# A pre-norm linear-attention block with a feed-forward layer: other engines, another order and other constants for its front half

## Chip, cores and metric

The kernel runs on one core of one Trainium2 chip. The metric is device time in microseconds (us); the time of a kernel is the median of its runs. The core's engines each take their instructions in the order in which the program lists them: TensorE (PE, matmuls), VectorE (DVE), ScalarE (ACT), GpSimd (POOL), and SyncE (SP), which here only issues DMAs.

## What is computed

```python
x: [1, 2048, 640] bf16        # H = 32 heads of 20
qkv = layernorm(x) @ wqkv     # [640, 1920]
pq, pk = q @ w_phi[h], k @ w_phi[h]                  # 20 x 20 for each head
phi_q = concat(softmax(pq), softmax(-pq)); phi_k likewise
kv = phi_k^T v;  z = sum over s of phi_k             # per head, 40 x 20 and 40
o  = (phi_q @ kv) / (phi_q @ z + 1e-6)
h  = x + o @ wo
out = h + silu(layernorm(h) @ w1) @ w2               # w1 [640, 1728], w2 [1728, 640]
```

## The kernel before

The 2048 rows are 16 tiles `t` of 128 rows. Weights and the whole of `X` stay in SBUF.

**Front.** `w_phi` is folded into the projections first: `phi_blocks` lays the 32 blocks of 20x20 along a diagonal in PSUM (37 small matmuls), `phi_a` and `phi_b` copy them to SBUF, `wk0`, `wk2`, `wk4` transpose `Wk` on PE, `wq0..4` transpose `Wq` by DMA, and `fold` multiplies them into `Wfk` and `Wfq`. Meanwhile `WARM` matmuls on a constant keep PE at work.

**Key phase, for each tile.** `st` (moments of the rows, DVE), `rs` (inverse deviation, POOL), `xn` (normalized rows; DVE for tiles below `XP`, else POOL), `xt` (transposed into `XnT`: on PE with a copy on ACT for tiles below `XD`, else a DMA transpose that SP issues), then `K` (project, PE), `ex` (exponentials, ACT), `su` (their sums, DVE), `rk` (1/sum, ACT), `sc` (scaling, DVE), `V` (project, PE), `ve` (copy, ACT) and `kv` (accumulate in one PSUM tile, PE). `bd0`, `bd1` cut the block diagonal out of it (DVE, with masks built on POOL). The query projections `Q` need `XnT` and `Wfq` alone.

**Attention, for each tile.** `qe` (ACT), `qs` and `qr` (DVE), `qt` (DMA transpose), `D` (PE), `E` (divide, DVE), `ot` (transpose: PE for the first two tiles, then DMA), `G` (output projection, PE), `ga` (residual, DVE), `ls`, `lr`, `hn` (second layer norm), `ht` (transpose).

**Feed-forward, for each tile.** `u` (up, PE), `s` (silu, ACT), `d` (down, PE), `oa` (residual, DVE), `out` (DMA). It starts once all query exponentials are done (`use_late`).

**What sets the order.** No order is written out. Each step is given to `Plan.add` with an engine, an assumed duration, a rank, what it depends on, an earliest time `after` and, for a DMA, an assumed time to landing `lands`. `Plan.run` goes through an imagined time and, of the steps that could begin, takes the one that can begin first (within `SLACK`), by rank among equals; it adds `HOP` between dependent steps. The instructions are emitted in that order, so these numbers decide only the order in each engine's queue. `AHEAD` bounds by how many tiles `D` may run ahead of the feed-forward.

Of the kernel before, what the change touches and what calls it, by code (L numbers as in the profile page):

```python
# [90 lines left out]
def kernel(  # L91
# [77 lines left out]
    nc.sync.dma_start(Wk[:, 0:3], wqkv_v[:, 0:3, D : 2 * D])  # L169
# [57 lines left out]
    def warm():  # L227

        nc.tensor.matmul(  # L229
            kv_ps[:, 0, :], ident[:], ident[:].unsqueeze(1).to_broadcast([P, 4, P]),  # L230
            start=True, stop=True,
        )
# [37 lines left out]
    PA = 380  # L270
    PN = 820
    HEADS = {0: (0, 7), 4: (25, 7), 1: (6, 7), 3: (19, 7), 2: (12, 8)}

    PB = {0: (0, 240, 0), 4: (400, 640, 140), 1: (120, 260, 380), 3: (380, 520, 520), 2: (240, 400, 660)}

    phi = early.tile([P, PN], BF16, name="phi")
    ps_of = {}

    def phi_blocks():
        pp = ps_of["phi"] = ps_pair()  # L280
        nc.tensor.matmul(pp[:, 0, 140:240], SID[:, 0:P], WPH[:, 0:5, :], start=True, stop=True)
        for r, (h0, n) in HEADS.items():
            for h in range(h0, h0 + n):
                at = DH * h - PB[r][0] + PB[r][2]
                b, at = (0, at) if at < PA else (1, at - PA)
                p0 = DH * h - P * r
                nc.tensor.matmul(
                    pp[:, b, at : at + DH], SID[:, P - p0 : 2 * P - p0], WPH[:, h, :],
                    start=True, stop=True,
                )  # L290
# [113 lines left out]
    for t in range(T):  # L404
        ahead = t - 3.2 if t > 0 else -10
        add(f"st{t}", "DVE", 1.06, 10 + ahead, [], lambda t=t: moments(t), after=AT_X[t])
        add(f"rs{t}", "POOL", 0.8, 10 + ahead, [f"st{t}"], lambda t=t: inv_std(t))
        ring = [f"xt{t - 4}"] if t > 3 else []
        if t < XP:
            add(f"xn{t}", "DVE", 0.42, 10 + ahead, [f"rs{t}"] + ring, lambda t=t: normal(t, nc.vector))  # L410
        else:
# [7 lines left out]
        else:  # L419
            add(  # L420
                f"xt{t}", "SP", 1.21, 10 + ahead, [f"xn{t}"],
                lambda t=t: nc.sync.dma_start_transpose(xt(t), xn_.pop(t)[:]), lands=2.6,
            )
            add(f"x{t}", "none", 0.0, 0, [f"xt{t}"], lambda: None)
            if later_loads:
                load = later_loads.pop(0)
                add(f"load{t}", "SP", 0.58, 10 + t, [f"xt{t}"], lambda load=load: nc.sync.dma_start(*load))
# [445 lines left out]
```

## Time and profile before

| | us |
|---|---|
| median of 3 runs (lowest to highest) | 255.53 (253.95 to 257.6) |
| the profiled execution's own time | 254.95 |
| its span, first to last instruction | 253.2 |
| busy in that span: PE, DVE, ACT, POOL | 240.1, 168.3, 109.0, 66.2 |
| granted TensorE clock, mean | 0.998 |

A group's row gives busy time, mean duration of one in ns, and the idle time of its engine just before it with what ended that. A timeline row gives start, duration, engine, line, operation, and in brackets the idle time before it. The chain of work is followed back from the last instruction, at each step to what released it.

### The profile page before, as it was taken

Reading aid. Unit: us, or ns where it says so; the run is one execution under the profiler, and the core shown is the slowest. Engines: PE = TensorE matmul, PEld = TensorE weight load, DVE = VectorE, ACT = ScalarE, POOL = GpSimd, SP = SyncE. Lnnn points to the kernel's source line nnn. Section 1 sums busy time; section 2 is a strip of 40 time slices with the busy share of each in tenths; the row PEclk is TensorE's granted clock in tenths of the full one; section 3 lists DMA queues with packets and bytes.
Section 4 is the critical chain, followed back from the end, with each engine's and each line's share of the span. In section 5 each row is a group of like instructions: output and inputs, shape, how many; then the busy total and the mean of one; then the engine's idle time right before and its main releaser. Section 6 shows DMA issues by size and latency. Waiting matters only on the chain.

```text
span 253.2 us, 6387 instructions
## 1 busy us (share of the span) xinstructions
PE 240.1 (95%) x2689; PEld 192.5 (76%) x2689; DVE 168.3 (66%) x349; ACT 109.0 (43%) x220; POOL 66.2 (26%) x103
## 2 busy tenths in 40 slices
PE   7989898989999899899999999999999999999994
PEld 3966566757677677797897897897898798797972
DVE  2698799895679889898968668667826526502011
ACT  2686676768689757640141141141141141041320
POOL 3269979999600011110200200200200100100000
PEclk9999999999999999999999999999999999999999
DMA  7997974673102825468465267485153213200001
GB/s 201 381 298 219 227 249 86 181 218 54 26 3 52 106 52 67 91 109 127 102 109 107 54 62 149 54 100 111 44 96 72 52 46 63 52 28 28 26 5 49
DMA packets 61302, 26.32 MB, mean 104 GB/s; under 512 B 53786, under 2 KB 60122, under 8 KB 61146
## 3 DMA queue, kind: packets, MB, share of 16 engines
q1 hardware_dynamic: 60624, 25.90, 48.3%
q8 instruction: 21, 0.34, 0.6%
q10 hardware_dynamic: 650, 0.03, 0.2%
q14 instruction: 7, 0.06, 0.1%
HBM read 10.35 MB, written 2.62 MB: 51 GB/s over the span
## 4 chain that ended last, share of the span: by engine, by line
PE 68%; POOL 17%; DMA 6%; ACT 5%; DVE 2%; issue 1%; POOLq 0%; ACTq 0%
PE half L781 24%; PE half L797 23%; POOL xn L386 13%; PE half L671 8%; ACT Eq L463 4%; DMA OT<-O 4%; PE pair L435 3%; PE half L640 3%; DMA XnT<-xn 2%; POOL rs L382 2%; PE half L446 2%; PE kv L229 2%; POOL rs L379 1%; PE pair L303 1%; PE pair L335 1%
## 5 line engine op out<-in xcount | busy, mean ns | idle before, releaser
L791 ACT ACTIVATE shT<-half 128x512 bf16<-128x512 f32 (+1 forms) x64 | 34.7, 544 | 107.9 <-PE half L781 107.9
L781 PE MATMUL half<-HnT,w_sb 128*128 128x128 bf16 x1120 | 66.0, 219 | 0.0
L781 PEld LDWEIGHTS <-w_sb 128*128 128x128 bf16 x1120 | 63.9, 98 | 1.1
L797 PE MATMUL half<-w_sb,shT 128*128 128x320 bf16 x448 | 64.8, 299 | 0.0
L797 PEld LDWEIGHTS <-shT 128*128 128x128 bf16 x448 | 43.0, 98 | 15.7
L435 PEld LDWEIGHTS <-XnT 128*128 128x128 bf16 x360 | 33.7, 98 | 19.2 <-DMA XnT<-xn 6.6
L379 POOL TENSOR_SCALAR rs<-mv 128x1 f32<-128x1 f32 x32 | 9.0, 282 | 148.8 <-DVE mv L375 148.7
L806 DVE TENSOR_TENSOR o_t<-half,X 128x320 bf16<-128x320 f32 x32 | 15.6, 486 | 35.3 <-PE half L797 35.3
L386 POOL TENSOR_SCALAR xn<-X,mv,rs 128x640 bf16<-128x640 bf16 x12 | 32.6, 2722 | 0.2
L374 DVE BATCH_NORM_STATS2 st<-X 128x6 f32<-128x320 bf16 x64 | 28.0, 480 | 4.5 <-DMA X<-in_A_x_dram 4.5
L435 PE MATMUL pair<-Wfk,XnT 128*128 128x320 bf16 x160 | 24.3, 299 | 5.0 <-DMA XnT<-xn 3.5
L478 DVE TENSOR_REDUCE Sk<-Ek 128x64 f32<-128x1280 bf16 x16 | 23.4, 1469 | 5.0 <-ACT Ek L463 5.0
L463 ACT ACTIVATE Ek<-pair 128x640 bf16<-128x640 f32 x32 | 20.7, 699 | 12.2 <-PE pair L435 12.1
L671 PE MATMUL half<-wo_sb,OT 128*128 128x320 bf16 x160 | 24.2, 299 | 1.3 <-DMA OT<-O 1.3
L573 DVE TENSOR_REDUCE Sq<-Eq 128x64 f32<-128x1280 bf16 x16 | 23.5, 1477 | 0.9 <-ACT Eq L463 0.9
L435 PE MATMUL pair<-Wv,XnT 128*128 128x320 bf16 x150 | 22.8, 299 | 0.0
L671 PEld LDWEIGHTS <-OT 128*128 128x128 bf16 x160 | 15.3, 98 | 7.7 <-DMA OT<-O 1.9
L678 DVE TENSOR_TENSOR X<-half,X 128x320 bf16<-128x320 f32 x32 | 15.3, 485 | 6.8 <-PE half L671 6.8
L650 DVE RECIPROCAL Rd<-half 128x16 f32<-128x16 f32 x32 | 7.9, 247 | 17.7 <-PE half L640 17.6
L382 POOL TENSOR_TENSOR rs<-rs,nhalf_t 128x1 f32<-128x1 f32 x32 | 18.2, 569 | 2.7
L463 ACT ACTIVATE Eq<-half 128x320 bf16<-128x320 f32 x48 | 16.7, 469 | 4.4 <-PE half L446 3.4
L446 PE MATMUL half<-Wfq,XnT 128*128 128x320 bf16 x120 | 17.4, 299 | 0.0
(68 smaller groups left out, 195.4 us busy)
## 6 DMA issues: line engine op xcount, KB each, us to landing
out_dram<-o_t SPq DMA_DIRECT2D x16, 160.0 KB, 2.0
w_sb<-in_B_w_dram SPq DMA_DIRECT2D x5, 432.0 KB, 4.5
w_sb<-in_B_w_dram SPq DMA_DIRECT2D x3, 480.0 KB, 4.3
X<-in_A_x_dram SPq DMA_DIRECT2D x1, 1280.0 KB
Wv<-in_A_wqkv_dram SPq DMA_DIRECT2D x1, 800.0 KB, 7.0
Wq<-in_A_wqkv_dram SPq DMA_DIRECT2D x1, 800.0 KB, 8.9
wo_sb<-in_A_wo_dram SPq DMA_DIRECT2D x1, 800.0 KB, 5.2
X<-in_A_x_dram SPq DMA_DIRECT2D x2, 320.0 KB, 5.5
```

What stands on the lines that cost most here:

```text
L374: nc.vector.bn_stats(st[:, i, :], X[:, t, i * HD : (i + 1) * HD])
L382: nc.gpsimd.tensor_tensor(rs_[t][:], rs_[t][:], nhalf_t[:], op=ALU.pow)
L386: eng.tensor_scalar(out=xn_[t][:], in0=X[:, t, :], scalar1=mv_.pop(t)[:, 0:1], scalar2=rs_.pop(t)[:], op0=ALU.subtract, op1=ALU.mult,)
L435: nc.tensor.matmul(ps[:, g, 0:HD], XnT[:, c, t * P : (t + 1) * P], W[:, c, g * HD : (g + 1) * HD], start=(c == 0), stop=(c == C - 1),)
L446: nc.tensor.matmul(ps[:, 0:HD], XnT[:, c, t * P : (t + 1) * P], W[:, c, g * HD : (g + 1) * HD], start=(c == 0), stop=(c == C - 1),)
L463: nc.scalar.activation(E5[:, g, :, b, :], p4, AF.Exp, scale=sign)
L478: nc.vector.tensor_reduce(sk[t][:], ek[t][:].rearrange("p (q f) -> p q f", f=DH), axis=AX.X, op=ALU.add)
L573: nc.vector.tensor_reduce(sq[t][:], eq[t][:].rearrange("p (q f) -> p q f", f=DH), axis=AX.X, op=ALU.add)
L671: nc.tensor.matmul(ps[:, 0:HD], ot[t][:, c, :], wo_sb[:, c, g * HD : (g + 1) * HD], start=(c == 0), stop=(c == C - 1),)
L781: nc.tensor.matmul(p3[:, i, :], w1_sb[:, c, fc * P : fc * P + P], HnT[u][:, c, 0:n], start=(c == 0), stop=(c == C - 1),)
L791: nc.scalar.activation(shT[u][:, f0:f1, 0:n], p3, AF.Silu)
L797: nc.tensor.matmul(ps[:, 0:HD], shT[u][:, fc, k * P : (k + 1) * P], w2_sb[:, fc, g * HD : (g + 1) * HD], start=(fc == 0), stop=(fc == FC - 1),
```

## The change

- POOL's list of normalizations loses two tiles: `xn` of tiles 6 and 11 joins tiles 0 to 3 on DVE. (The short description speaks of four tiles; two change the engine of `xn`, and two more, tiles 2 and 3, have `xt` on PE and ACT instead of a DMA.)
- The 11 loads of `wo`, `w1` and `w2` no longer hang one by one behind the `xt` DMAs; each gets an assumed earliest time of 30 us, 33 us and so on.
- `phi` is made by six matmuls (a replicated identity `REP` times up to eight heads at once), and DVE multiplies the result by a 0/1 mask `own` while it takes it out of PSUM. POOL builds `own`; before, ACT did the two copies.
- `Wk`'s first three chunks are loaded by ACT's queue, behind `w_phi`, instead of SP's.
- The warm-up multiplies a tile set by DVE and not the identity that POOL makes; ten of them instead of nine.
- `Plan`'s numbers change: DMA transposes are assumed to land after 4.7 us (2.6 and 2.7 before; 5.5 instead of 3.5 for `qt`) and to hold SP for 1.6 us (1.21), `HOP` is 0.23 (0.15), `SLACK` 0.05 (0.1), POOL's `xn` 2.75 (2.5), and the ranks of `E`, `ga` and `oa`, `AHEAD` (3.7 to 3.02) and `QLAG` (2 to 1) move.

```diff
-    SLACK = 0.1
-    HOP = 0.15
+    SLACK = 0.05
+    HOP = 0.23
...
+    LEAD = 2.5
+    LAND = 4.7
+    XDVE = (0, 1, 2, 3, 6, 11)
+    LOADS = (30.0, 3.0)
+    XD = 4
+    ROFF = (-4, -9, -5)
...
     nc.scalar.dma_start(WPH[:], A_w_phi.rearrange("h d f -> d h f"))
+    nc.scalar.dma_start(Wk[:, 0:3], wqkv_v[:, 0:3, D : 2 * D])
...
     load_x(0, 2)
-    nc.sync.dma_start(Wk[:, 0:3], wqkv_v[:, 0:3, D : 2 * D])
...
+    warm_t = early.tile([P, 4 * P], BF16, name="warm_t")
+    nc.vector.memset(warm_t[:], 1.0)
...
+    REP = early.tile([DH, H, DH], BF16, name="REP")
+    nc.gpsimd.tensor_copy(REP[:], ident[0:DH, 0:DH].unsqueeze(1).to_broadcast([DH, H, DH]))
...
+    own = early.tile([P, NB, 8, DH], BF16, name="own")
+    nc.gpsimd.memset(own[:], 1.0)
+    nc.gpsimd.affine_select(
+        out=own[:], in_=own[:], compare_op=ALU.is_ge, fill=0.0,
+        base=0, pattern=[[4, NB], [-DH, 8], [0, DH]], channel_multiplier=1,
+    )
...
+                nc.tensor.matmul(
+                    pp[:, i // 3, at : at + n * DH], rep[:, r * P : (r + 1) * P], WPH[:, h0 : h0 + n, :],
+                    start=True, stop=True,
+                )
...
+        nc.vector.tensor_tensor(
+            phi[:, 3 * b : 3 * b + n, 0 : 8 * DH],
+            ps_of["phi"][:, b, 0 : 8 * DH * n].rearrange("p (i f) -> p i f", i=n),
+            own[:, 3 * b : 3 * b + n].rearrange("p i h f -> p i (h f)"), op=ALU.mult,
+        )
...
-        if t < XP:
+        if t in XDVE:
...
-                f"xt{t}", "SP", 1.21, 10 + ahead, [f"xn{t}"],
-                lambda t=t: nc.sync.dma_start_transpose(xt(t), xn_.pop(t)[:]), lands=2.6,
+                f"xt{t}", "SP", 1.6, 10 + ahead, [f"xn{t}"],
+                lambda t=t: nc.sync.dma_start_transpose(xt(t), xn_.pop(t)[:]), lands=LAND,
             )
             add(f"x{t}", "none", 0.0, 0, [f"xt{t}"], lambda: None)
-            if later_loads:
-                load = later_loads.pop(0)
-                add(f"load{t}", "SP", 0.58, 10 + t, [f"xt{t}"], lambda load=load: nc.sync.dma_start(*load))
+    for i, load in enumerate(later_loads):
+        add(f"load{i}", "SP", 1.2, 50, [], lambda load=load: nc.sync.dma_start(*load), after=LOADS[0] + LOADS[1] * i)
```

Three places show what this does to the queues. The first is SP's queue between the loads of the start and the middle of the key phase, before:

```order
L326 DMA_TRANSPOSE WTq<-Wq 128x5x128 x2
L422 DMA_TRANSPOSE XnT<-xn 128x5x128 x2
L326 DMA_TRANSPOSE WTq<-Wq 128x5x128
L427 DMA wo_sb<-in_A_wo_dram 128x5x640
L427 DMA w_sb<-in_B_w_dram 128x1728
L422 DMA_TRANSPOSE XnT<-xn 128x5x128
L326 DMA_TRANSPOSE WTq<-Wq 128x5x128 x2
L422 DMA_TRANSPOSE XnT<-xn 128x5x128
L427 DMA w_sb<-in_B_w_dram 128x1728 x2
```

The same place of SP's queue after the change:

```order
L362 DMA_TRANSPOSE WTq<-Wq 128x5x128 x4
L458 DMA_TRANSPOSE XnT<-xn 128x5x128
L362 DMA_TRANSPOSE WTq<-Wq 128x5x128
L458 DMA_TRANSPOSE XnT<-xn 128x5x128 x3
L463 DMA wo_sb<-in_A_wo_dram 128x5x640
L463 DMA w_sb<-in_B_w_dram 128x1728
```

The first `XnT` transpose is now tile 4's (tiles 2 and 3 have left the queue), and no load of a weight stands ahead of those of tiles 4 to 7. The second place is POOL's queue from tile 5 on (`rs_394` and `xn_414` are tile 5's), before:

```order
L386 TENSOR_SCALAR xn_414<-X_80,mv_342,rs_394 128x640
L379 TENSOR_SCALAR rs_464<-mv_416 128x1
L382 TENSOR_TENSOR rs_464<-rs_464,nhalf_t_101 128x1
L256 MEMSET w2_sb_79 64x640
L386 TENSOR_SCALAR xn_499<-X_80,mv_416,rs_464 128x640
L379 TENSOR_SCALAR rs_531<-mv_480 128x1
L382 TENSOR_TENSOR rs_531<-rs_531,nhalf_t_101 128x1
L257 MEMSET mask_108 128x420
L386 TENSOR_SCALAR xn_557<-X_80,mv_480,rs_531 128x640
```

POOL's queue from tile 5 on after the change:

```order
L422 TENSOR_SCALAR xn_401<-X_80,mv_323,rs_373 128x640
L415 TENSOR_SCALAR rs_453<-mv_393 128x1
L418 TENSOR_TENSOR rs_453<-rs_453,nhalf_t_102 128x1
L267 MEMSET w2_sb_79 64x640
L415 TENSOR_SCALAR rs_475<-mv_456 128x1
L418 TENSOR_TENSOR rs_475<-rs_475,nhalf_t_102 128x1
L268 MEMSET mask_109 128x420
L422 TENSOR_SCALAR xn_496<-X_80,mv_456,rs_475 128x640
```

Tile 6 keeps its `rs` there (`rs_453`) but its `xn` is gone, so that tile 7's `xn` follows that of tile 5. The third place is DVE's queue at the end of the key phase, before (`Sk` and `Ek` are the sums and scalings of the keys, `Sq` the first sums of a query tile, `KVB` the block diagonal):

```order
L478 TENSOR_REDUCE Sk<-Ek 128x64
L491 TENSOR_TENSOR Ek<-Ek,Rk 128x1280
L478 TENSOR_REDUCE Sk<-Ek 128x64
L491 TENSOR_TENSOR Ek<-Ek,Rk 128x1280
L573 TENSOR_REDUCE Sq<-Eq 128x64
L519 TENSOR_TENSOR KVB<-kv,mask 128x5x84
```

DVE's queue there after the change:

```order
L609 TENSOR_REDUCE Sq<-Eq 128x64
L514 TENSOR_REDUCE Sk<-Ek 128x64
L617 RECIPROCAL Rq<-Sq 128x32
L619 TENSOR_TENSOR Rho<-Sq,Rq 128x64
L626 TENSOR_TENSOR Eq<-Eq,Rho 128x32x20
L514 TENSOR_REDUCE Sk<-Ek 128x64
L527 TENSOR_TENSOR Ek<-Ek,Rk 128x1280
L514 TENSOR_REDUCE Sk<-Ek 128x64
L527 TENSOR_TENSOR Ek<-Ek,Rk 128x1280 x2
L514 TENSOR_REDUCE Sk<-Ek 128x64 x2
L527 TENSOR_TENSOR Ek<-Ek,Rk 128x1280 x2
L609 TENSOR_REDUCE Sq<-Eq 128x64 x2
```

The sums of query tile 0 (`Sq`) now stand ahead of the last five key sums, and the rest of its work (`Rq`, `Rho`, `Eq`) ahead of the last four; before, all of it came behind them. On PE, four query projections (`Q0` to `Q3`) now stand ahead of the last `kv`, where there were two.

More of the change, by code (lines that the diff above doesn't have):

```diff
@@ L152, in ps_half_bf16 @@
         return pools["half"].tile([P, 8, P], BF16, name="half")
+    ST1 = 4.9
+    ST2 = 10.4
+    ST3 = 12.8
+    WARM = 10
+    LEAD = 2.5
+    V0 = 3.25
+    WQ = 14.0
+    LAND = 4.7
+    XDVE = (0, 1, 2, 3, 6, 11)
+    LOADS = (30.0, 3.0)
+    XD = 4
+    NE = 4
+    EQT = 3
+    RAMP = 2
+    QSUM = (20, 22, 24)
+    QLAG = 1
+    AHEAD = 3.02
+    NHN = 4
+    NSH = 4
+    ROFF = (-4, -9, -5)
     Wk = early.tile([P, C, D], BF16, name="Wk")
@@ L229, in warm @@
         nc.tensor.matmul(
-            kv_ps[:, 0, :], ident[:], ident[:].unsqueeze(1).to_broadcast([P, 4, P]),
-            start=True, stop=True,
+            kv_ps[:, 0, :], warm_t[:, 0:P], warm_t[:], start=True, stop=True,
         )
     for i in range(WARM):
-        add(f"warm{i}", "PE", 0.42, 3 * R, [], warm, after=1.4)
+        add(f"warm{i}", "PE", 0.42, 3 * R, [], warm, after=1.0)
     for i, v in enumerate(VP):
@@ L269 @@
     NB = 5
[L270 to L276, printed above, removed]
+    BW = 240
+    BLOCKS = (0, 3, 1, 4, 2)
+    HEAD0 = {0: 0, 3: 19, 1: 6, 4: 25, 2: 12}
+    PB = {
+        0: (0, 240, 0), 3: (380, 520, BW), 1: (120, 260, 2 * BW), 4: (400, 640, 3 * BW - 100),
+        2: (240, 400, 4 * BW),
+    }
+    assert all(P * r - DH * HEAD0[r] == 4 * i for i, r in enumerate(BLOCKS))
+    phi = early.tile([P, NB, BW], BF16, name="phi")
+    own = early.tile([P, NB, 8, DH], BF16, name="own")
[4 more added lines that the diff above has]
+    )
+    nc.gpsimd.affine_select(
+        out=own[:], in_=own[:], compare_op=ALU.is_ge, fill=0.0,
+        base=DH - 1, pattern=[[-4, NB], [DH, 8], [0, DH]], channel_multiplier=-1,
+    )
+    nc.gpsimd.memset(phi[:, :, 8 * DH : BW], 0.0)
     ps_of = {}
@@ L280, in phi_blocks, with phi_own @@
         pp = ps_of["phi"] = ps_pair()
[L281 to L286, printed above, removed]
+        rep = REP[:].rearrange("k h d -> k (h d)")
+        for i, r in enumerate(BLOCKS):
+            at = 8 * DH * (i % 3)
+            for h0, n in [(HEAD0[r], min(8, H - HEAD0[r]))] + [(0, 1)] * (HEAD0[r] + 8 > H):
                 nc.tensor.matmul(
-                    pp[:, b, at : at + DH], SID[:, P - p0 : 2 * P - p0], WPH[:, h, :],
+                    pp[:, i // 3, at : at + n * DH], rep[:, r * P : (r + 1) * P], WPH[:, h0 : h0 + n, :],
                     start=True, stop=True,
                 )
-    add("phi", "PE", 1.2, 1, [], phi_blocks, after=AT_WPH, ring=("pair", [["phi_a", "phi_b"]]))
-    add("phi_a", "ACT", 0.5, 1, ["phi"], lambda: act(phi[:, 0:PA], ps_of["phi"][:, 0, 0:PA]))
-    add("phi_b", "ACT", 0.5, 1.1, ["phi"], lambda: act(phi[:, PA:PN], ps_of["phi"][:, 1, 0 : PN - PA]))
+                at += n * DH
+    def phi_own(b):
+        n = 3 - b
+        nc.vector.tensor_tensor(
[3 more added lines that the diff above has]
+        )
+    add("phi", "PE", 0.6, 1, [], phi_blocks, after=AT_WPH, ring=("pair", [["phi_a", "phi_b"]]))
+    add("phi_a", "DVE", 0.6, 1, ["phi"], lambda: phi_own(0))
+    add("phi_b", "DVE", 0.45, 1.1, ["phi"], lambda: phi_own(1))
     Wfk = proj.tile([P, C, D], BF16, name="Wfk")
```

48 lines of the change are left out of this document (17 added, 31 removed).

## Prediction

> **What bounds the kernel now.** First the totals and the chain of work on the profile's page:
>
> ```profile
> span 253.2 us, 6387 instructions
> ...
> PE 240.1 (95%) x2689; PEld 192.5 (76%) x2689; DVE 168.3 (66%) x349; ACT 109.0 (43%) x220; POOL 66.2 (26%) x103
> ...
> PE 68%; POOL 17%; DMA 6%; ACT 5%; DVE 2%; issue 1%; POOLq 0%; ACTq 0%
> ```
>
> PE works in 240.1 of 253.2 us, so all that better order can give back is the 13.1 us in which it doesn't. Yet 17% of the chain lies on POOL, which is busy for a quarter of the span: there must be a stage that POOL bounds. A table of stages shows where (columns: stretch and length, then busy us and instructions of PE, PE's weight loads, DVE, ACT and POOL):
>
> ```profile
> 4.53:13.84 9.31, 9.07 (x116) 7.77 (x115) 6.94 (x17) 5.44 (x9) 2.56 (x6) 1.00 1.05 380
> 13.84:55.70 41.86, 37.29 (x348) 27.06 (x347) 37.23 (x64) 30.27 (x62) 37.63 (x38) 1.00 0.84 211
> 55.70:73.00 17.30, 16.25 (x158) 12.07 (x159) 11.49 (x11) 12.33 (x26) 11.41 (x15) 1.00 0.17 30
> 73.00:104.00 31.00, 29.01 (x260) 21.41 (x258) 26.93 (x60) 24.94 (x61) 1.61 (x4) 1.00 0.46 68
> 104.00:216.00 112.00, 111.54 (x1408) 94.97 (x1406) 78.51 (x185) 26.71 (x49) 10.29 (x26) 1.00 0.49 84
> 216.00:249.90 33.90, 33.82 (x403) 28.20 (x400) 6.81 (x17) 8.03 (x15) 0.79 (x2) 1.00 0.11 30
> ```
>
> PE's idle time is length minus PE busy: 0.24, 4.57, 1.05, 1.99, 0.46 and 0.08 us. So 5.6 us lie in the key phase (13.84 to 73.00), 2.0 in the ramp of the attention, half a microsecond in 146 us of feed-forward. The rest is the start (1.42 us) and the last output (3.3), which the change leaves. PE's timeline names the waits (start, duration, then in brackets the idle time and what ended it):
>
> ```profile
> 27.46 1.53 PE L435 MATMUL pair<-Wfk,XnT 128*128 128x320 bf16 x10 [1.25 <-DMA XnT<-xn]
> ...
> 42.36 1.53 PE L435 MATMUL pair<-Wfk,XnT 128*128 128x320 bf16 x10 [1.16 <-ACT Wfq L344]
> ...
> 56.02 1.53 PE L435 MATMUL pair<-Wfk,XnT 128*128 128x320 bf16 x10 [1.10 <-DMA XnT<-xn]
> ...
> 86.85 0.62 PE L640 MATMUL half<-KVB,EqT 128*128 128x126 bf16 x10 [1.16 <-ACT OT L666]
> ...
> 102.44 1.53 PE L671 MATMUL half<-wo_sb,OT 128*128 128x320 bf16 x10 [0.81 <-DMA OT<-O]
> ...
> 173.53 1.53 PE L671 MATMUL half<-wo_sb,OT 128*128 128x320 bf16 x10 [0.46 <-DMA OT<-O]
> ```
>
> Most end with a DMA transpose that landed late, because its input or its turn on SP came late. All these are waits in the queue's order: PE had other work, but behind.
>
> **The start: -0.3 us.** The chain's first pieces, one piece of the ramp to compare with, and the load that is moved:
>
> ```profile
> 1.42 3.60 PE kv L229 x8
> 5.01 0.20 PE pair L281
> 5.21 0.95 PE pair L287 x36
> 6.16 0.54 PE kv L229
> 6.70 2.13 PE pair L303 x20
> 8.83 0.53 PE pair L393 x5
> ...
> 90.19 0.28 PE half L393 x5
> ```
>
> ```profile
> 1.25 0.42 SPq L169 DMA_DIRECT2D Wk<-in_A_wqkv_dram  x1
> ```
>
> ```profile
> Wk<-in_A_wqkv_dram SPq DMA_DIRECT2D x1, 480.0 KB, 4.7
> ```
>
> Eight warm-up matmuls of 512 columns took 3.60 us, 0.45 each or 0.88 ns a column. The 37 small `phi` matmuls (0.20 + 0.95 = 1.15) become six with 5 x 160 = 800 columns: 0.70. Ten warm-ups take 4.5 us and begin when DVE has filled their tile, between 0.7 us earlier than the 1.42 of now (half of what stands before it) and no earlier; so `phi` would end between 5.9 and 6.6, where the ninth warm-up ended at 6.70. But `Wk`'s first chunks landed at 1.25 + 4.7 = 5.95, and are issued behind `w_phi` now and share the DMA engines with `X`: between 5.9 and 7.2 (all of one 480 KB load at the same rate). I take 0.3 us gained, between a gain of 0.8 and a loss of 0.5. The two copies of `phi` leave ACT and become 800 columns of multiplication on DVE; DVE's share is priced below. POOL's masks stand ahead of `rs` of tile 0:
>
> ```profile
> masks.py:199 POOL TENSOR_SCALAR_AFFINE_SELECT ident<-ident 128x128 bf16<-128x128 bf16 x1 | 0.3, 294 | 0.1
> ...
> L244 POOL TENSOR_SCALAR_AFFINE_SELECT mask<-mask 128x84 f32<-128x84 f32 x5 | 1.4, 284 | 0.0
> ```
>
> ```profile
> 5.75 0.22 POOL L379 TENSOR_SCALAR rs<-mv 128x1 f32<-128x1 f32 x1 [3.15 <-DVE mv L375]
> ```
>
> No row shows a POOL operation of 800 elements. From 84 elements in 284 ns to 128 in 294 gives 0.45 us by the slope, in proportion to the second 1.84. The five new ones (a copy, two fills, two selects) take between 2.2 and 9.2 us. POOL stood idle for 3.15 us ahead of tile 0's `rs`, and the chain has that tile's transpose on PE only at 8.83, some two us after its rows are ready: cover for 5.2 us. I take the slope, being what both rows together say, and cost nothing; the upper end loses 4.0.
>
> **The key phase: -4.4 us.** What POOL does and what moves (groups: busy, mean ns of one):
>
> ```profile
> L386 POOL TENSOR_SCALAR xn<-X,mv,rs 128x640 bf16<-128x640 bf16 x12 | 32.6, 2722 | 0.2
> ...
> L573 DVE TENSOR_REDUCE Sq<-Eq 128x64 f32<-128x1280 bf16 x16 | 23.5, 1477 | 0.9 <-ACT Eq L463 0.9
> ...
> L651 DVE TENSOR_TENSOR O<-half,Rd 128x320 bf16<-128x320 f32 x32 | 15.7, 492 | 1.1
> ...
> L386 DVE TENSOR_SCALAR xn<-X,mv,rs 128x640 bf16<-128x640 bf16 x20 | 8.8, 438 | 1.1 <-POOL rs L382 1.1
> ...
> L590 DVE TENSOR_TENSOR Eq<-Eq,Rho 128x640 bf16<-128x640 bf16 x16 | 7.9, 492 | 0.6
> ...
> L581 DVE RECIPROCAL Rq<-Sq 128x32 f32<-128x32 f32 x16 | 5.5, 342 | 0.1
> ...
> L583 DVE TENSOR_TENSOR Rho<-Sq,Rq 128x64 bf16<-128x64 f32 x16 | 3.6, 225 | 0.5
> ```
>
> ```profile
> 17.32 2.52 POOL L386 TENSOR_SCALAR xn<-X,mv,rs 128x640 bf16<-128x640 bf16 x1
> ...
> 60.55 3.73 POOL L386 TENSOR_SCALAR xn<-X,mv,rs 128x640 bf16<-128x640 bf16 x1
> ```
>
> POOL's first `xn` begins at 17.32 and its last ends at 64.28: 47 us for 12 tiles. Two fewer take 2 x 2.72 = 5.4 us off, so its last would end near 58.8. Then POOL no longer ends last, and what does? DVE. Its idle time, from the same table, is 2.37 + 4.63 + 5.81 = 12.81 us up to 73.00, where its last key scaling ends. It gets more work before that point: two `xn` (0.88), the mask multiplication (800 columns from PSUM at 492 ns for 320: 1.23), and the whole of query tile 0 (1.477 + 0.342 + 0.225 + 0.492 = 2.54), together 4.65 us. What stays of the 12.81? The 5.81 behind 55.70 fall where POOL was last: gone. Of the 7.0 before it, I let 0.5 go with the late transpose at 27.46 and keep 6.5. Then the last scaling comes 12.81 - 6.5 - 4.65 = 1.7 us earlier, and PE has by then done two query projections more, of ten matmuls, each some 1.36 us (a row's 1.53 less the 0.17 us by which the last overlaps the next): 2.7. Sum 4.4. PE itself sets a cap of 5.6 - 0.56 = 5.0, with two tiles' transposes more at 0.28 each. The bounds are 5.0 gained and the loss of the slower rival below.
>
> The SP queue carries this:
>
> ```profile
> 20.48 0.57 SPq L427 DMA_DIRECT2D wo_sb<-in_A_wo_dram  x1
> 21.10 0.52 SPq L427 DMA_DIRECT2D w_sb<-in_B_w_dram  x1
> 21.72 1.47 SPq L422 DMA_TRANSPOSE XnT<-xn  x1
> ```
>
> ```profile
> XnT<-xn SPq DMA_TRANSPOSE x14, 3.0
> ```
>
> Tile 4's rows were ready at 19.84 (17.32 + 2.52), but its transpose was issued at 21.72, behind a `Wq` transpose and two loads, and PE's wait of 1.25 us ended at 27.46. After, four `Wq` transposes end ahead of it and no load stands there: issued at about 20, it lands at 23 to 25.7 (after the median 3.0 or the 5.7 of now). PE asks for it near 24.5: the first key projection begins where the second stage of the table does, at 13.84, and seven projections of 1.36 us, two tiles' transposes and some small matmuls come before tile 4's. The 11 loads still pass SP ahead of tiles 8 to 15; POOL's lead of up to 5 us is their cover, and without it each would cost its 0.5 to 0.6 us of issue. The weights are first read in the ramp, behind 73.
>
> **Ramp and feed-forward: -1.3 us.** Query tile 0 is ready before the key phase ends, so the first attention no longer waits for its sums, ratio and DMA. But DVE was busy for 26.93 of 31 us there, and two first sums (3.0 us) now stand ahead of the block diagonal. I take half of PE's 1.99 us, between all of it and a loss of 1.0 (one more wait like that at 86.85). In the feed-forward I take 0.3 of 0.46, since more of PE's work now stands between a tile's `D` and its `G`. Bounds: 0.46 gained, 1.0 lost.
>
> **The sum.** -0.3 - 4.4 - 1.0 - 0.3 = -6.0 us: the profiled execution of 254.95 (253.2 and 1.75 around it) would give 248.95. It stands 0.58 under the median of 255.53, so by the median **249.5**, 2.3% less. The lowest and highest run lie 1.4% apart, so 2% (250.4 and 260.6) is about what can be told.
>
> **Rivals.**
> - *DVE takes POOL's place* (20%). More of its waits are for ACT (`ex`, `rk`) than for POOL; the full queue of moments then puts them off. With 9.0 us idle instead of 6.5 the key phase gives 1.9, the ramp nothing: 255.53 - 0.3 - 1.9 = 253.3. For it: between 13.84 and 55.70 DVE is busy in 89% already. Against it: PE has four projections as filler.
> - *The array speeds up earlier* (13%). The 20 transposes from 6.70 took 107 ns each; the same five in the ramp take 0.28, 56 ns each. If the many small `phi` matmuls kept the rate low, an unbroken train of ten would raise it before the 25 `Wk` transposes: 25 x 51 ns = 1.3 us more, 248.2. Against it: eight large ones in 3.6 us didn't. The Trainium skill, "TensorE: Matmul & The Clock Gate", section "Part 1: The HAM clock gate", says that the array goes to full rate after about 3.4 us of sustained work in a window that runs freely; the trace agrees only if `phi` counts as a break, and by the rule this case would be the likely one.
> - *The gaps only move* (7%). Landings, not their assumed length, are late: four `Wq` transposes in a row now stand ahead of tile 4's. With the 1.25 us and the like kept and only 1.0 gained: 254.5.
> - *Slower* (5%). One mechanism, in DVE's queue: all its 12.81 us of idle time stay, being ACT's round trips. The 4.65 us more push the last scaling back by as much, and PE's filler gives back 2.7: 255.53 + 1.9 = 257.4. It decides from 12.81 - 4.65 + 2.7 = 10.9 us of idle time on.
>
> **Chances and range.** The forecast has 55%, with its own range 247.9 to 251.2; four fifths of it lie under 250.4. Faster by over 2%: 0.44 + 0.13 = 0.57. Slower by over 2%: 0.03, beyond the slower rival's own time. The rest, 0.40, is within. The range 246.5 to 253.6 takes in the forecast, the array's earlier speed with all of the key phase's cap, and DVE's case; the last two rivals stay out.
>
> **What would show it.** Right: POOL's last `xn` ends near 59 and PE's idle time between 13.84 and 73 is under 2 us; the last `kv` matmuls start near 72 with four query projections done; DVE's idle time up to its last key scaling is 6 to 7 us; feed-forward is as dense as now. Wrong: PE waits for `Ek` scalings (DVE) instead of transposes; `rs` of tile 0 begins after 8 us; the `Wk` transposes run at 56 ns; or PE waits for `OT` again and again behind 104.

## The result and the profile after

| | before | changed |
|---|---|---|
| median of 6 runs, us (lowest to highest) | 254.33 (253.53 to 257.6) | 245.91 (245.57 to 246.99) |
| the profiled execution, us | 254.95 | 245.69 |
| its span, us | 253.2 | 244.0 |

The ratio is 0.968 (95% interval 0.9642 to 0.9717): 8.4 us faster by the medians, 9.3 between the two profiled executions. The forecast was 6.0 faster, 249.5, with a range from 246.5: right in direction, too small in size. The ratio and its interval leave out the run of 257.6, more than 1.5% above the fastest of its kernel; without it the median of before is 253.95 and the gain 8.0.

The same rows of the page as before, now of the changed kernel:

```profile
span 244.0 us, 6342 instructions
...
PE 236.8 (97%) x2669; PEld 191.3 (78%) x2669; DVE 170.7 (70%) x354; ACT 107.1 (44%) x216; POOL 64.1 (26%) x104
...
PE 94%; DMA 2%; DVE 1%; ACT 1%; ACTq 0%; issue 0%
```

POOL's 17% of the chain is gone altogether, though POOL's busy time fell only from 66.2 to 64.1 us. PE's is 94% where it was 68%. The table of stages of the changed kernel (length, then PE, PE's weight loads, DVE, ACT, POOL):

```profile
4.51:13.59 9.08, 7.25 (x86) 5.56 (x84) 7.68 (x19) 4.44 (x7) 4.09 (x12) 1.00 1.07 388
13.59:73.00 59.41, 58.91 (x567) 44.32 (x567) 55.71 (x84) 47.89 (x98) 43.77 (x50) 1.00 0.64 158
73.00:104.00 31.00, 31.00 (x322) 24.55 (x321) 28.85 (x69) 21.98 (x54) 3.17 (x8) 1.00 0.43 81
104.00:216.00 112.00, 112.00 (x1414) 95.63 (x1412) 71.61 (x169) 26.39 (x49) 8.67 (x22) 1.00 0.46 81
```

PE's idle time in the key phase went from 5.62 to 0.50 us, in the ramp from 1.99 to 0.00, in the feed-forward from 0.46 to 0.00. All waits of PE that its timeline still shows before the last output:

```profile
1.51 3.98 PE L241 MATMUL kv<-warm_t 128*128 128x512 bf16 x10 [1.51 <-DVE warm_t L215]
7.33 1.29 PE L339 MATMUL pair<-ident,Wk 128*128 128x128 bf16 x20 [1.38 <-DMA Wk<-in_A_wqkv_dram]
9.37 1.55 PE L371 MATMUL pair<-phi,WTk 128*128 128x240 bf16 x18 [0.19 <-DVE WTk L355]
13.59 1.52 PE L471 MATMUL pair<-Wfk,XnT 128*128 128x320 bf16 x10 [0.24 <-DVE Wfk L380]
32.78 0.56 PE L543 MATMUL kv<-VP,Ek 128*128 128x84 bf16 x10 [0.45 <-DVE Ek L527]
```

From 33 us on PE never waits for data until the end. The longest wait that the kernel before did not have is at 7.33, for the load that was moved to ACT's queue.

**What a wait costs beside its idle time.** The three stages' idle time fell by 7.6 us, the start came 0.25 us earlier, and two more tiles' transposes on PE took 0.56: that makes 7.3 of the 9.2 us of span. Two rows of the changed kernel's timeline, one behind the other, show where more went:

```profile
69.02 1.52 PE L471 MATMUL pair<-Wfq,XnT 128*128 128x320 bf16 x10
70.38 0.55 PE L543 MATMUL kv<-VP,Ek 128*128 128x84 bf16 x10
```

The projection lasts 1.52 us by its row, but the next group begins after 1.36: successive matmuls overlap by 0.16 us in the profile, where the ends of matmuls are modelled, and that much stands as busy time ahead of every wait. Eleven waits of before behind 13.84 became one, which by this estimate is 10 x 0.16 = 1.6 us, so 8.9 of 9.2 are told; the last 0.3 is not.

### The profile page after: what moved, and what is told of

It is laid out like the page before. It is cut to its first block, busy times and chain, and to the rows that moved or that the text cites. A ratio compares the mean times of both kernels' runs of the same rounds, so it can differ in the third digit from the quotient of the medians.

```text
span 244.0 us, 6342 instructions
## 1 busy us (share of the span) xinstructions
PE 236.8 (97%) x2669; PEld 191.3 (78%) x2669; DVE 170.7 (70%) x354; ACT 107.1 (44%) x216; POOL 64.1 (26%) x104
## 4 chain that ended last, share of the span: by engine, by line
PE 94%; DMA 2%; DVE 1%; ACT 1%; ACTq 0%; issue 0%
PE half L817 26%; PE half L833 25%; PE pair L471 20%; PE half L707 9%; PE half L482 6%; PE half L676 3%; PE kv L543 3%; DMA Wk<-in_A_wqkv_dram 2%; PE pair L371 1%; PE kv L471 1%; ACT Ek L499 1%; PE half L429 0%; DVE Wfk L380 0%; DVE Ek L527 0%; PE pair L339 0%; ACT WTk L355 0%
## 5 line engine op out<-in xcount | busy, mean ns | idle before, releaser
L817 PE MATMUL half<-HnT,w_sb 128*128 128x128 bf16 x1120 | 66.9, 219 | 0.0
L833 PE MATMUL half<-w_sb,shT 128*128 128x320 bf16 x448 | 63.5, 299 | 0.0
L415 POOL TENSOR_SCALAR rs<-mv 128x1 f32<-128x1 f32 x32 | 7.6, 238 | 154.3 <-DVE mv L411 154.3
L471 PEld LDWEIGHTS <-XnT 128*128 128x128 bf16 x380 | 36.2, 98 | 13.5 <-issue 0.5
L422 POOL TENSOR_SCALAR xn<-X,mv,rs 128x640 bf16<-128x640 bf16 x10 | 27.9, 2790 | 0.1
L418 POOL TENSOR_TENSOR rs<-rs,nhalf_t 128x1 f32<-128x1 f32 x32 | 19.0, 594 | 2.7
L687 DVE TENSOR_TENSOR O<-half,Rd 128x320 bf16<-128x320 f32 x32 | 15.7, 491 | 1.1
L499 ACT ACTIVATE Eq<-half 128x320 bf16<-128x320 f32 x40 | 14.0, 458 | 3.0 <-PE half L482 3.0
L482 PE MATMUL half<-Wfq,XnT 128*128 128x320 bf16 x100 | 14.7, 299 | 0.0
```

Of the source, the lines that this page charges most:

```text
L418: nc.gpsimd.tensor_tensor(rs_[t][:], rs_[t][:], nhalf_t[:], op=ALU.pow)
L422: eng.tensor_scalar(out=xn_[t][:], in0=X[:, t, :], scalar1=mv_.pop(t)[:, 0:1], scalar2=rs_.pop(t)[:], op0=ALU.subtract, op1=ALU.mult,)
L471: nc.tensor.matmul(ps[:, g, 0:HD], XnT[:, c, t * P : (t + 1) * P], W[:, c, g * HD : (g + 1) * HD], start=(c == 0), stop=(c == C - 1),)
L482: nc.tensor.matmul(ps[:, 0:HD], XnT[:, c, t * P : (t + 1) * P], W[:, c, g * HD : (g + 1) * HD], start=(c == 0), stop=(c == C - 1),)
L499: nc.scalar.activation(E5[:, g, :, b, :], p4, AF.Exp, scale=sign)
L817: nc.tensor.matmul(p3[:, i, :], w1_sb[:, c, fc * P : fc * P + P], HnT[u][:, c, 0:n], start=(c == 0), stop=(c == C - 1),)
```

## Experiments

Times are medians; the ratio is to the kernel before, run on the same chip. "Waits" means the sum of PE's waits behind the first key projection, in key phase, ramp and feed-forward (before: 5.5, 2.0, 0.5; changed: 0.45, 0, 0).

### The two halves of the change, each alone

The kernel before with tiles 6 and 11 normalized on DVE:

```diff
-        if t < XP:
+        if t < XP or t in (6, 11):
```

> The kernel before with one part of the change: tiles 6 and 11 are normalized on DVE. Theory A (POOL's rate of one normalization per 3.9 us bounded the key phase): most of that phase's loss goes, POOL's last normalization ends near 59 us, 249.5 us against 254.3. Theory B (the order was wrong because landings were assumed too short): PE still meets late transposes in its queue, no more than 1.5 us gained, 253.

251.89 us, 0.992 (0.9889 to 0.9948). Waits 3.7, 0.5, 1.1. That is between the two theories (249.5 and 253). POOL lost two tiles, its last `xn` ended at 62.4 instead of 64.28, and PE still met late tiles.

The kernel before with all of the plan's numbers:

```diff
-    SLACK = 0.1
-    HOP = 0.15
+    SLACK = 0.05
+    HOP = 0.23
...
-            add(f"xn{t}", "POOL", 2.5, 10 + ahead, [f"rs{t}"] + ring, lambda t=t: normal(t, nc.gpsimd))
+            add(f"xn{t}", "POOL", 2.75, 10 + ahead, [f"rs{t}"] + ring, lambda t=t: normal(t, nc.gpsimd))
...
-                lambda t=t: nc.sync.dma_start_transpose(xt(t), xn_.pop(t)[:]), lands=2.6,
+                lambda t=t: nc.sync.dma_start_transpose(xt(t), xn_.pop(t)[:]), lands=LAND,
...
```

with SP's holds, `LEAD` (it shifts the ranks of a tile's normalization), the rank and earliest time of `wq`, `QLAG`, `AHEAD` and `ROFF` (the ranks of `E`, `ga` and `oa`) as in the change.

> The kernel before with one part of the change: the plan's numbers alone (landing 4.7 us, hop, slack, durations of SP and POOL, ranks of E, ga, oa, AHEAD, QLAG, LEAD). Theory A: POOL still ends last in the key phase (64 us), only the 2.0 us of the ramp and the 0.5 us of the feed-forward go, with their refills 3 us: 251.3. Theory B: the order fills the key phase's waits with query projections too: 248.

249.5 us, 0.983 (0.9769 to 0.9889). Waits 2.0, 1.4, 0. No work went to another engine, and PE, DVE and POOL run as many instructions as before. ACT runs eight fewer (212 for 220): a query tile that is projected before the PSUM buffers are divided anew gets its exponentials in two instructions and not in four, and four more tiles are. So beside the order in the queues the numbers decide this too. They gain 4.3 us, where relieving POOL gains 1.9. Up to 1.2 of the 4.3 can be the start's (first key projection at 12.62 in this profile, 13.84 before; the array's rate, below); the kernel with the assumed times alone, further down, gains 4.2 without such help.

Both together, without the new `phi`, without tiles 2 and 3 on PE, with `Wk` on SP, the weights' loads behind the `xt` DMAs and the warm-up as before:

> The kernel before with all of the plan's numbers and tiles 6 and 11 normalized by DVE; phi, the loads, XD = 2 and the warm-up as before. Theory 'each part pays for itself on top of the right order': the numbers' 249.5 less 1 to 2, 247.5 to 248.5. Rival 'the numbers had already taken what the tiles on DVE give, and only tiles 2 and 3 on PE pay': 249 to 250. Rival 'the two belong together and the rest is nothing': 246 to 247.

248.76 us, 0.980 (0.9756 to 0.9841). The waits left behind the start (engine, line, what it waited for: sum, times, longest):

```profile
PE kv L509 <- DVE Ek L493: 2.2, 2, 1.3
...
PE pair L337 <- DMA WTq<-Wq: 1.0, 1, 1.0
```

No `XnT` is late any more; what is late is DVE, and one transpose of `Wq`. Its median lies 0.7 under the numbers alone, but the two profiles differ in the start too (first key projection at 13.83 and 12.62, for the array's rate, below): behind it, the one took 233.0 us to the end of its span and the other 235.0.

### Taken from the changed kernel one by one

```diff
-    XDVE = (0, 1, 2, 3, 6, 11)
+    XDVE = (0, 1, 2, 3)
```

> The changed kernel with tiles 6 and 11 normalized on POOL again. Theory A: POOL bounds the key phase again, 4 to 5 us are lost: 250.5 against 245.9. Theory B: query projections fill what POOL leaves open, at most 1 us is lost: 247.

248.59 us, 0.979 (0.9738 to 0.9848): 2.7 more than the changed kernel, between the two theories (250.5 and 247). PE's waits behind the start are not for POOL's tiles:

```profile
PE half L482 <- ACT Eq L499: 1.4, 1, 1.4
PE kv L543 <- DVE Ek L527: 1.0, 1, 1.0
```

```diff
-    XD = 4
+    XD = 2
```

> The changed kernel with tiles 2 and 3 transposed by DMA again and not on PE and ACT. Theory (they kept PE's start of the key phase dense, at 0.56 us of PE's own time): the waits for Wq's and XnT's DMAs between 18 and 20 us come back, 1.0 us lost net, 247. Rival (the query work fills it): 0.5 us gained, 245.4.

248.55 us, 0.979 (0.9744 to 0.9829): 2.6 more. Waits 3.1, 0, 0, of which 2.2 for DVE's `Ek` scalings and 0.7 for ACT.

The plan's numbers of before in the changed kernel (the second diff above, reversed; the landing of `xt` goes to 2.7, where before it was 2.6):

> The changed kernel with the plan's numbers of before (landing 2.7 us, hop, slack, durations of SP and POOL, ranks, AHEAD, QLAG, LEAD). Theory A: the ramp's and the feed-forward's waits come back, 3 us: 249. Theory B: those of the key phase too: 251.5.

253.33 us, 0.997 (0.9935 to 0.9997): 7.4 more, nearly all of the gain, with POOL's ten tiles, the new `phi` and the four transposes on PE in place. Waits 3.6, 1.9, 0.5; the largest are

```profile
PE pair L471 <- DMA XnT<-xn: 2.5, 3, 1.2
PE half L429 <- DVE xn L422: 1.9, 1, 1.9
```

The loads of `wo`, `w1` and `w2` chained one by one behind the `xt` DMAs again:

```diff
-    for i, load in enumerate(later_loads):
-        add(f"load{i}", "SP", 1.2, 50, [], lambda load=load: nc.sync.dma_start(*load), after=LOADS[0] + LOADS[1] * i)
...
+            if later_loads:
+                load = later_loads.pop(0)
+                add(f"load{t}", "SP", 0.58, 10 + t, [f"xt{t}"], lambda load=load: nc.sync.dma_start(*load))
```

> The changed kernel with the loads of wo, w1 and w2 hanging one by one behind the DMA transposes of XnT again. Theory A (the late loads matter little, since the order by then has the transposes far ahead of need): at most 1 us lost, 246.5. Rival (loads ahead of the transposes of tiles 4 to 7 were what made them late): the waits near 20 and 27 us come back, 2 to 3 us lost, 248.5.

246.27 us, 0.971 (0.967 to 0.9752), span 244.0 like the changed kernel's, no new wait. Where the loads stand is worth nothing that these runs tell.

### Which of the numbers

The landing alone, in the kernel before (4.7 at all transposes, 5.5 for `qt`):

```diff
-                lambda t=t: nc.sync.dma_start_transpose(xt(t), xn_.pop(t)[:]), lands=2.6,
+                lambda t=t: nc.sync.dma_start_transpose(xt(t), xn_.pop(t)[:]), lands=4.7,
...
```

> The kernel before with one number changed: DMA transposes are assumed to land after 4.7 us (5.5 for the query tiles) instead of 2.6 to 2.7 (3.5). Theory B: most of the 4.3 us that all the new numbers gained: 250.5 against 253.8. Rival: at most 1 us, 253.

252.84 us, 0.997 (0.9948 to 0.9994): the rival was right. Waits 4.5, 1.4, 0. And taken back in the changed kernel:

```diff
-    LAND = 4.7
+    LAND = 2.7
```

> The changed kernel with one number changed: DMA transposes are assumed to land after 2.7 us (3.5 for the query tiles) instead of 4.7 (5.5). Theory B (this number is what removed PE's waits): most of the 7.4 us that all the old numbers cost come back, 251. Rival (the ranks of E, ga and oa, AHEAD, LEAD and the hop do it together, or the hop and SP's longer hold): at most 2 us lost, 247.5.

249.44 us, 0.984 (0.9796 to 0.9881): 3.5 more than the changed kernel, between theory and rival. Waits 1.7, 1.0, 0.

Next, each in the kernel before, the numbers of the second diff in two lots: all assumed times (landing, SP's hold, POOL's durations, `HOP`, `SLACK`), no rank; and all ranks and limits (`LEAD`, rank and earliest time of `wq`, `QLAG`, `AHEAD`, `ROFF`), no time:

> The kernel before with half of the plan's new numbers: the assumed times (landing 4.7 and 5.5 us, SP's hold 1.6 and 2.35, POOL's 0.87 and 2.75, hop 0.23, slack 0.05), no rank. Theory C (the plan must know how late the whole chain POOL, SP, landing is; the landing alone gained 0.6): most of the 4.3 us that all the numbers gained, 250.5 against 253.6. Rival (the ranks do it): as with the landing alone, 252.8.

249.53 us, 0.982 (0.978 to 0.9858). Waits 1.4, 1.4, 0; its first key projection is at 14.05, so that none of the 4.2 us is the start's.

> The kernel before with the other half: ranks and limits (LEAD, wq behind the tiles and not before 14 us, QLAG, AHEAD, ROFF), no assumed time. Theory C: little alone, 252.5 to 253. Rival: most of the 4.3 us, 250. If both halves gain little, it is their product: a rank decides only where the plan sees two steps ready, and it sees that wrongly with the old times.

253.88 us, 1.001 (0.9979 to 1.0043). Waits 5.3, 0.9, 0.8. So the times carry the numbers' gain. Which of them? Four more kernels with a part of these edits. Without the landing:

```diff
-    HOP = 0.15
+    HOP = 0.23
...
-                f"xt{t}", "SP", 1.21, 10 + ahead, [f"xn{t}"],
+                f"xt{t}", "SP", 1.6, 10 + ahead, [f"xn{t}"],
...
```

> The kernel before with the plan's assumed times of the change except the landing (how long a transpose holds SP, POOL's durations, HOP, SLACK; landing stays 2.6 and 2.7). All times together gave 0.982, the landing alone 0.997. Theory 'the landing is the necessary part, the others help only with it': 252 to 254, PE's waits on XnT stay. Rival 'the SP hold and POOL's durations are what was wrong': 249.5 to 250.5.

248.63 us, 0.979 (0.9741 to 0.984). Waits 2.8, 1.3, 0.7; its profile has the first key projection at 12.36, so that of its 5.2 us up to 1.5 are the start's. The landing and SP's hold alone:

> The kernel before with landing 4.7/5.5 and the hold of SP 1.6 (2.35 for query transposes), POOL's durations, HOP and SLACK as before. Theory 'what counts is the whole path from a transpose's issue to its use': near all times together, 249.5 to 250.5. Rival 'POOL's 2.75 instead of 2.5 is needed too, since twelve of them add up to 3 us late in the plan': 251.5 to 253, with PE's waits on XnT late in the key phase, where POOL has fallen behind the plan.

253.62 us, 0.999 (0.9961 to 1.0012). Waits 3.5, 3.1, 0. POOL's durations alone:

```diff
-            add(f"xn{t}", "POOL", 2.5, 10 + ahead, [f"rs{t}"] + ring, lambda t=t: normal(t, nc.gpsimd))
+            add(f"xn{t}", "POOL", 2.75, 10 + ahead, [f"rs{t}"] + ring, lambda t=t: normal(t, nc.gpsimd))
...
```

> The kernel before with POOL's assumed times alone: xn 2.75 instead of 2.5, rs and lr 0.87 instead of 0.8. Landing and hold together gave 0.999; all times without the landing gave 0.979. Theory 'the old plan took POOL for faster than it is (twelve xn at 2.72 us in the trace), so it put tiles too early into PE's queue': 249 to 251. Rival 'HOP and SLACK do it': 253 to 254.5, no change.

253.7 us, 0.999 (0.9966 to 1.0018). Waits 5.6, 3.4, 0.9. `HOP` and `SLACK` alone:

> The kernel before with HOP 0.23 for 0.15 and SLACK 0.05 for 0.1 alone. Theory 'POOL's assumed times do it': 253 to 254.5. Rival 'HOP, the step from one engine to the next that stands some eight times in a tile's chain from moments to kv, does it': 249 to 251. Both half way would mean that any change that makes the plan's chain longer does.

252.48 us, 0.993 (0.9907 to 0.9949). Waits 5.4, 0.4, 0.5; its first key projection is at 12.72, so that all of its 1.4 us can be the start's.

Both of my theories fell: neither the landing nor POOL's durations is the one number. By the medians the landing alone gives 0.6 us, POOL's durations 0.2, hop and slack 1.4, landing and hold together 0.3, but all four groups 4.2 and all but the landing 5.2. What each profile takes behind its first key projection leaves the start out (one profile each, that of before from a run 0.6 us above its median): before 239.4 us, ranks alone 239.5, POOL's durations 240.5, hop and slack 238.2, landing and hold 237.8, landing 236.9, all but the landing 235.5, all numbers 235.0, all times 233.4.

The pair that tells most is all times against landing and hold, each with twelve `xn` on POOL. POOL's row (shortest, median, longest in ns, then first and last start) of the kernel with all times, then of the one with landing and hold:

```profile
L386 POOL TENSOR_SCALAR xn<-X,mv,rs x12: 2506/2520/3155, 17.5 to 56.8; 128x640 bf16<-128x640 bf16 x12
```

```profile
L386 POOL TENSOR_SCALAR xn<-X,mv,rs x12: 2513/2518/3802, 17.4 to 56.7; 128x640 bf16<-128x640 bf16 x12
```

And PE's largest waits behind the start in the same two kernels, in that order:

```profile
PE half L446 <- ACT Eq L463: 1.4, 1, 1.4
PE pair L435 <- DMA XnT<-xn: 0.6, 1, 0.6
PE pair L335 <- DMA WTq<-Wq: 0.4, 1, 0.4
PE kv L507 <- DVE Ek L491: 0.4, 1, 0.4
```

```profile
PE pair L435 <- DMA XnT<-xn: 1.4, 2, 1.2
PE half L446 <- ACT Eq L463: 1.4, 1, 1.4
PE kv L507 <- DVE Ek L491: 1.2, 2, 0.8
PE half L393 <- DVE xn L386: 0.9, 1, 0.9
PE half L393 <- ACT HnT L701: 0.8, 1, 0.8
```

POOL's `xn` are the same twelve, the first and the last within 0.1 us, and the kernels lie 4.1 us apart. In the slower of the two POOL's last `xn` are

```profile
54.15 5.02 POOL L386 TENSOR_SCALAR xn<-X,mv,rs 128x640 bf16<-128x640 bf16 x2
```

They end at 59.17, where the kernel before with the same twelve tiles ended at 64.28. The forecast wanted 58.8 from taking two tiles away; here POOL is as early without that, and the time is that of before. Its waits in the key phase did fall, from 5.5 to 3.5 us, but those of the ramp grew from 2.0 to 3.1.

POOL's old durations (2.5 and 0.8) put into the changed kernel:

> The changed kernel with POOL's assumed times as before (2.5 and 0.8). Theory 'POOL's assumed times matter only where POOL is late, and with ten tiles it no longer is': 245.5 to 246.5, no new wait of PE. Rival 'the plan is only tuned as a whole, any number back costs': 247 to 250, with waits of PE on XnT or Ek.

249.38 us, 0.981 (0.9762 to 0.985). The rival was right: POOL is no longer late and the number still counts. Part of it is the start. Of its four executions two had a mean granted clock of 0.998 and 1.0 (248.3 and 248.47, so some 2.5 us go to order), two of 0.991 and 0.993 (250.28 and 250.31); the profiled one is of the latter, and the section on what the chip showed has its rows.

### The start

`Wk`'s first chunks on SP again:

```diff
-    nc.scalar.dma_start(Wk[:, 0:3], wqkv_v[:, 0:3, D : 2 * D])
...
     load_x(0, 2)
+    nc.sync.dma_start(Wk[:, 0:3], wqkv_v[:, 0:3, D : 2 * D])
```

> The changed kernel with Wk's first chunks issued by SP again, behind the first X load; the order on every other engine is the same. Theory A (the move to ACT's queue cost time: the chunks landed 5.9 us after issue instead of 4.7, and PE waited 1.38 us for them): they land near 6.0 us, PE's wait goes, the first key projection begins near 12.7 instead of 13.59, and the run is 0.9 us faster: 245.0. Rival (the start is bounded by the copies on DVE and ACT and by the arrival of X and Wv): no change, 245.9.

245.0 us (244.88 to 245.75), 0.966 (0.9632 to 0.9696). This is the best version run. Its interval overlaps the changed kernel's, so the two aren't told apart by time; the profiles tell them apart. Issue to landing in the changed kernel, then in this one:

```profile
Wk<-in_A_wqkv_dram ACTq DMA_DIRECT2D x1, 480.0 KB, 5.9
```

```profile
Wk<-in_A_wqkv_dram SPq DMA_DIRECT2D x1, 480.0 KB, 4.7
```

And PE's timeline in this one:

```profile
6.01 1.33 PE L339 MATMUL pair<-ident,Wk 128*128 128x128 bf16 x20
7.17 0.44 PE L339 MATMUL kv<-ident,Wk 128*128 128x128 bf16 x5
7.99 0.45 PE L429 MATMUL pair<-ident,xn 128*128 128x128 bf16 x5 [0.37 <-DVE phi L322]
...
12.45 1.52 PE L471 MATMUL pair<-Wfk,XnT 128*128 128x320 bf16 x10 [0.24 <-DVE Wfk L380]
```

The transposes start 1.3 us earlier, the first key projection 1.14 us earlier, and 0.7 us of it is left at the end.

The same with the old `phi` (37 small matmuls, copies on ACT, no masks):

> The changed kernel with Wk's first chunks on SP's queue and with phi as before (37 small matmuls, two copies on ACT, no mask). Theory D (phi's masks only matter at the start, where DVE now holds the first transpose by 0.37 us): PE takes 0.6 us longer for phi but Wk lands at 6.0 anyway; the same as with Wk on SP alone, 245.0. Rival (the small matmuls delay the array's full rate): the Wk transposes run at 107 ns each again, 1.3 us lost, 246.3.

248.71 us, 0.979 (0.9755 to 0.983): 3.7 more than with `Wk` on SP alone, where the rival gave 1.3. The transposes took 2.31 us for 20 and the first key projection began at 14.41. The rest of its loss lies in the ramp (2.2 us of waits), where the order changed with `phi`; which of its pieces did that was not tried.

## Why the forecast fell short, step by step

**The step that failed** is the reading "there must be a stage that POOL bounds", with its price: "47 us for 12 tiles. Two fewer take 2 x 2.72 = 5.4 us off", and from there "Then POOL no longer ends last, and what does? DVE". That POOL stood in the chain was read from the profile; that it set the pace of the key phase was only argued. The runs show otherwise. Taking the two tiles off POOL alone gained 1.9 us; the numbers alone, with all twelve tiles on POOL, gained 4.3, the assumed times among them 4.2; and in the pair with equal POOL rows twelve tiles took 42 us and not 47, at two times 4.1 us apart. So the larger part is the order of the queues, and not POOL's rate.

POOL got its 17% because PE stood before the last late tile. What stood behind it in PE's queue, before the change:

```profile
66.93 1.53 PE L435 MATMUL pair<-Wfk,XnT 128*128 128x320 bf16 x10 [0.40 <-DMA XnT<-xn]
...
70.04 0.56 PE L335 MATMUL pair<-phi,WTq 128*128 128x240 bf16 x6
70.44 0.71 PE L435 MATMUL pair<-Wfq,XnT 128*128 128x320 bf16 x4
```

At 70.04 is the last piece of the fold that makes `Wfq`, and at 70.44 the first query projection, which needs it. The transposes of `Wq` were all issued by 24.6 us and none took longer than 6.3 to land, so the last piece's input had lain there for 39 us; until it was done PE had no query projection to put into its waits. In the changed kernel:

```profile
42.48 0.56 PE L371 MATMUL pair<-phi,WTq 128*128 128x240 bf16 x6
...
49.07 1.52 PE L471 MATMUL pair<-Wfq,XnT 128*128 128x320 bf16 x10
```

The forecast did say that PE "had other work, but behind", and then priced the stage by POOL's tiles and DVE's idle time all the same. Whether the earlier fold is what the gain comes from is not shown: in the equal pair the faster kernel has its first query projection at 54.43 and the slower at 67.97, but the kernel with POOL's durations alone has it at 52.67 and gains nothing.

| term | forecast | measured |
|---|---|---|
| start | -0.3 | -0.25 |
| key phase | -4.4 | -5.7: 5.1 of idle time, 7 waits fewer at 0.16, less 0.56 of transposes |
| ramp | -1.0 | -2.3: all of 1.99, 2 waits fewer |
| feed-forward | -0.3 | -0.6: all of 0.46, one wait fewer |

These make 8.9 of the 9.2 us of span. Three mis-sizings, then:

- **The cap.** "PE itself sets a cap of 5.6 - 0.56 = 5.0" was not one: with the 0.16 us of each wait it is about 6.3, and the key phase gave 5.7.
- **The halves.** "I take half" of the ramp's idle time, and 0.3 of 0.46, had no row behind it. The two first sums do stand ahead of the block diagonal, as feared, but cost nothing; the last key scaling and what followed it on DVE are

```profile
67.12 1.57 DVE L527 TENSOR_TENSOR Ek<-Ek,Rk 128x1280 bf16<-128x1280 bf16 x2
69.05 2.88 DVE L609 TENSOR_REDUCE Sq<-Eq 128x64 f32<-128x1280 bf16 x2 [0.36 <-ACT Eq L499]
71.84 0.58 DVE L555 TENSOR_TENSOR KVB<-kv,mask 128x420 bf16<-128x420 f32 x1
```

  and PE, with query projections to do, reached the first `D` at 74.84 without a wait.
- **DVE's idle time.** The forecast had DVE "keep 6.5" of 12.81; the stages of the changed kernel (4.51:13.59, 13.59:55.70, 55.70:68.69) leave 1.40 + 0.87 + 2.44 = 4.7 us. The last scaling ends at 68.69, 4.3 us earlier than the 73.00 of before, where the sum had 1.7. DVE did take POOL's place as the engine that is late, but at a full 98% between 13.59 and 55.70 it cost PE one wait of 0.45.

**What held.** POOL's last `xn` was to end near 58.8:

```profile
55.27 2.57 POOL L422 TENSOR_SCALAR xn<-X,mv,rs 128x640 bf16<-128x640 bf16 x1
```

It ends at 57.84. PE's idle time in the key phase is under 2 us, four query projections are done when the last `kv` starts (70.38; forecast 72), and the feed-forward is dense. POOL's five new operations were to cost nothing:

```profile
2.94 1.16 POOL L295 TENSOR_SCALAR_AFFINE_SELECT own<-own 128x800 bf16<-128x800 bf16 x1
4.17 1.15 POOL L299 TENSOR_SCALAR_AFFINE_SELECT own<-own 128x800 bf16<-128x800 bf16 x1
...
5.90 0.39 POOL L415 TENSOR_SCALAR rs<-mv 128x1 f32<-128x1 f32 x1
```

They cost nothing, though a select took 1.15 us, half way between the bounds of 0.45 and 1.84; `rs` of tile 0 began at 5.90 instead of 5.75.

**The start was right by two errors.** The array did speed up earlier: 20 transposes in 1.29 us instead of 2.34. That rival had 13%, its sign came true (56 ns from one transpose to the next), and its 1.3 us were there; they went into the wait of 1.38 us for `Wk`, which landed 7.3 us into the span, just above the 5.9 to 7.2 allowed. With `Wk` back on SP they show at the end as 0.7 us.

**The rivals.** *DVE takes POOL's place* is one wait of 0.45 us in the changed kernel and counts only where other parts of the change are missing: with `XD` = 2, or without the two tiles on DVE, PE waits 2.2 and 1.0 us for DVE's `Ek`. *The gaps only move* did not happen: behind the moved `Wq` transposes no `XnT` is late. *Slower* appeared nowhere.

**What stays open.** No single assumed time carries the 4 us, and taking one back (landing, or POOL's durations) costs 2.5 to 3.5 of them. Whether these values are nearer the chip's, or one lucky order among many, these runs don't tell: no kernel with other values of like size was run. One row speaks against "nearer" for the landing, assumed at 4.7 for both, and one for it; in the changed kernel the transposes of `xn` landed after a median of 2.6 us, those of `Wq` after 4.3:

```profile
XnT<-xn SPq DMA_TRANSPOSE x12, 2.6
WTq<-Wq SPq DMA_TRANSPOSE x5, 4.3
```

The parts beside the numbers (tiles on DVE, tiles 2 and 3 on PE, the new `phi`) give 0.5 us together under the old numbers (253.81 to 253.33) and some 3.6 on top of the new ones (249.5 to 245.9); these runs don't divide that among them.

## To carry to other kernels

An engine in the chain of waits is not yet the bound: look at what stands behind the waiting instruction with its inputs there, and try the order alone before work is moved. Price a removed wait at its idle time plus the overlap that it breaks, here 0.16 us each. A list schedule's assumed times count as a set: here one or two of them alone gave next to nothing, and the same one taken away cost more than a per cent.
